# A linear-attention and mixture-of-experts kernel: logits for four blocks at once, routing in three parts, indirect transfers spread singly over the pairs, a PSUM bank of its own for each first-layer quarter

## The chip, the cores and the metric

The kernel runs on one core of a Trainium2 chip. The metric is the device time of one execution in microseconds (us). Three timed executions of the kernel before took 499.47, 500.51 and 506.63 us; the median is 500.51 us.

## The reference

Two stages follow each other. The first is causal linear attention with a decay per head, over 4 sequences of 768 tokens with 8 heads of 64. The second sends each of the 3072 tokens to the one of 8 experts with the highest logit, and weights what this expert gives by the softmax of that logit.

```
for b in range(nb):                       # blocks of 64 tokens
    intra = einsum('bhic,bhjc->bhij', qb, kb) * Dmask
    intra = einsum('bhij,bhjd->bhid', intra, vb)
    inter = einsum('bhid,bhde->bhie', qb * lam_pow, kv_state)
    out[:, :, sl] = intra + inter
    kv_state = lam_block * kv_state + einsum('bhsd,bhse->bhde', kb * rev_pow, vb)
logits = x @ w_gate + modality_bias[modality_id]
e_idx = argmax(logits, axis=1)
gate_w = softmax(logits)[arange(N), e_idx]
for e in range(E):                        # D = 512, F = 1024
    h = maximum(x[e_idx == e] @ w1[e], 0.0)
    out[e_idx == e] = gate_w[..., None] * (h @ w2[e])
```

With the inputs that are used, nearly all tokens go to two experts: 1319 to expert 3, 1494 to expert 6, 253 to expert 5 and 6 to expert 7.

## The kernel before

**Order.** The instructions of TensorE (PE), VectorE (DVE), ScalarE (ACT) and the queue engine SP stand in the order in which the program text issues them, and each engine executes its own in that order. GpSimd (POOL) has an order of its own that a list keeps (`pool(...)`). Indirect transfers are issued by POOL, one instruction per 128 rows.

**Attention.** The 24 blocks of 128 tokens go in 12 pairs, numbered m. For one pair PE computes `scores` (L245), the part from the running state (`from_state`, L284), the part from the values (`values`, L292), the update of the state (`products`, L257) and the logits (`gates`, L313). `gates` of one block issues 16 matmuls of 32 columns by 32 columns, each with a group of 32 tokens; a matmul on float32 shows as two records of the trace, so the two blocks of a pair show as x64.

**Routing.** The 24 blocks are routed in 4 parts of 6 blocks. For one part DVE transposes the logits (`lgt`, L326) and picks the expert (`choose`), PE counts ranks (`ranks`, L345 to L348), DVE works out slots (`slots_of`), and POOL scatters a record per token into a table `inv` in DRAM (`write_slots`, L375, one indirect transfer per block). After half of the tokens `count` (L383) and `early_list` fix two early tiles of 256 tokens; after all of them `late_list` fixes the rest.

**Experts.** A tile is 256 tokens of one expert. There are 2 early tiles, 2 thin tiles (64 and 32 tokens) and, with these inputs, 10 wide ones. For each tile SP fetches the tile's part of `inv` (`gidx`), POOL gathers the rows (`xg<-xs`, L551, 8 indirect transfers), DVE transposes them (`turn_rows`, L576), and ACT and DVE split rows and weights into a high and a low half (`split`, L524 and L525). `first_layer` has four quarters i of 24 matmuls (L588 to L590), each followed by a ReLU on ACT (`hh`, L606) and by the low half of its result on DVE (`hl`, L607). Two quarters share one PSUM tile `s` of two banks, of which there are two. `second` has 2 x 24 matmuls (L588 to L590, `o`), then ACT scales (`y`, L620) and POOL scatters the rows to the output (L621).

**The seam.** Behind the last pair the program issues `turn_rows` and `split_rows` of early tile 0, `choose` for the last part, the gathers of tile 1, the scatters, and then `first_layer` of tile 0. Its quarter 0 is followed by `rank_last`, which issues `ranks`, `slots_of`, the last scatters and `count`; quarters 1 to 3 stand behind them on PE. `keep_busy(18)` lets PE multiply zeros at the very start.

## Time and profile before

| | us |
|---|---|
| timed executions | 499.47, 500.51, 506.63 |
| profiled execution, device time | 502.24 |
| its span | 500.3 |
| PE busy | 404.7 (81%) |
| DVE busy | 265.1 (53%) |
| POOL busy | 218.3 (44%) |
| ACT busy | 204.7 (41%) |

The span is what the trace covers of the profiled execution; 1.94 us of its device time lie around it. Busy shares are means over stages that differ much. A matmul row of the timeline begins with its start; what stands in square brackets is the engine's idle time before it and what ended it, and "issue" is idle time for which the profile shows no wait.

### The profile page before, as it was taken

How to read it: one execution, taken by the hardware profiler on the slowest of the kernel's cores; microseconds unless marked ns; L12 is line 12 of the kernel's file. 1: busy time of each engine (PE TensorE's matmuls, PEld its weight loads, DVE VectorE, ACT ScalarE, POOL GpSimd, SP SyncE). 2: the span in 40 equal slices, each digit the busy share in tenths (PEclk: the TensorE clock that was granted, in tenths of full speed). 3: DMA queues.
4: the chain of work that ended last, by engine and by line, in shares of the span. 5: the costliest groups of instructions: out<-in, count | busy, mean ns of one | idle time of the engine just before them, and what ended most of it. 6: DMA issues, size and time to landing. Idle time of an engine off the chain costs nothing.

```text
span 500.3 us, 10978 instructions
## 1 busy us (share of the span) xinstructions
PE 404.7 (81%) x4118; PEld 353.8 (71%) x4118; DVE 265.1 (53%) x440; ACT 204.7 (41%) x385; POOL 218.3 (44%) x230
## 2 busy tenths in 40 slices
PE   8977887886518938958888889897979797989882
PEld 4867777775418838737777787787878787878871
DVE  4556667766134874206655545465656464747420
ACT  2744542661022512205444426354544444545320
POOL 1752555368725104561271808263635454450200
PEclk9998998996558969978999989899999999999998
DMA  7999992747100002940121856631111111010101
GB/s 262 400 411 409 412 412 89 256 96 246 37 8 2 22 22 36 284 153 10 12 63 19 262 154 202 182 82 42 33 53 23 63 20 67 17 63 3 43 3 38
DMA packets 39951, 62.67 MB, mean 125 GB/s; under 512 B 22730, under 2 KB 22732, under 8 KB 39888
## 3 DMA queue, kind: packets, MB, share of 16 engines
q1 hardware_dynamic: 29120, 42.83, 25.6%
q0 software_dynamic: 5936, 12.69, 7.9%
q10 hardware_dynamic: 4832, 6.36, 3.6%
q8 instruction: 34, 0.56, 0.5%
q14 instruction: 29, 0.24, 0.2%
HBM read 90.52 MB, written 13.67 MB: 208 GB/s over the span
## 4 chain that ended last, share of the span: by engine, by line
issue 39%; POOL 16%; DVE 4%; PE 4%; SPq 2%; DMA 2%; ACT 1%; another core or an unknown queue 1%; POOLq 1%; DVEq 0%; ACTq 0%
POOL xg L551 12%; POOL out_dram L621 4%; PE o L664 1%; SPq L536 1%; DVE w1l L525 1%; DMA xg<-xs,gidx 1%; PE s L588 1%; DMA gidx<-inv 1%; PE s L590 1%; PE s L589 1%; SPq L540 1%; POOLq L551 0%; DVE xt L576 0%; ACT w1h L524 0%
## 5 line engine op out<-in xcount | busy, mean ns | idle before, releaser
L551 POOL DMA_INDIRECT xg<-xs,gidx x80 | 99.1, 1239 | 118.7 <-DVE xt L576 90.0
L588 PE MATMUL s<-xh,w1h 128*128 128x256 f32 x384 | 115.8, 302 | 42.4 <-DVE hl L607 37.6
L589 PE MATMUL s<-xl,w1h 128*128 128x256 f32 x384 | 112.5, 293 | 2.0 <-issue 2.0
L588 PEld LDWEIGHTS s<-xh,w1h 128*128 128x128 f32 x384 | 77.3, 201 | 51.8 <-DVE hl L607 41.9
L590 PE MATMUL s<-xh,w1l 128*128 128x256 f32 x384 | 112.4, 293 | 0.5 <-issue 0.5
L525 DVE TENSOR_TENSOR w2l<-raw,w2h 128x1024 fp32r<-128x1024 f32 x48 | 58.8, 1225 | 38.4 <-ACT y L620 22.7
L590 PEld LDWEIGHTS s<-xh,w1l 128*128 128x128 f32 x384 | 77.5, 202 | 1.8 <-issue 1.8
L589 PEld LDWEIGHTS s<-xl,w1h 128*128 128x128 f32 x384 | 77.4, 201 | 1.9 <-issue 1.5
L606 ACT ACTIVATE hh<-s 128x512 fp32r<-128x512 f32 x48 | 28.7, 598 | 118.3 <-PE s L590 111.9
L607 DVE SCALAR_TENSOR_TENSOR hl<-s,hh 128x512 fp32r<-128x512 f32 x48 | 33.2, 691 | 80.4 <-ACT hh L606 76.2
L588 PE MATMUL o<-w2h,hh 128*128 128x512 f32 x192 | 75.0, 390 | 0.0
L590 PE MATMUL o<-w2h,hl 128*128 128x512 f32 x192 | 74.8, 390 | 0.0
L589 PE MATMUL o<-w2l,hh 128*128 128x512 f32 x192 | 74.7, 389 | 0.0
L525 DVE TENSOR_TENSOR w1l<-raw,w1h 128x1024 fp32r<-128x1024 f32 x48 | 57.0, 1247 | 2.8 <-issue 1.4
L524 ACT CAST w2h<-raw 128x1024 fp32r<-128x1024 f32 x48 | 49.8, 1037 | 0.0
L524 ACT CAST w1h<-raw 128x1024 fp32r<-128x1024 f32 x48 | 46.7, 1046 | 0.4 <-issue 0.4
L621 POOL DMA_INDIRECT out_dram<-y,idx x20 | 23.6, 1178 | 46.9 <-ACT y L620 42.0
L235 ACT ACTIVATE kd<-load,dk 128x64 f32<-128x64 f32 x160 | 39.6, 334 | 7.9 <-DVE state L274 3.8
L590 PEld LDWEIGHTS o<-w2h,hl 128*128 128x128 f32 x192 | 36.0, 188 | 7.7
L589 PEld LDWEIGHTS o<-w2l,hh 128*128 128x128 f32 x192 | 36.1, 188 | 7.1
L588 PEld LDWEIGHTS o<-w2h,hh 128*128 128x128 f32 x192 | 36.0, 188 | 7.0
L375 POOL DMA_INDIRECT inv<-pay,sloti x24 | 25.3, 1056 | 15.6 <-DVE sloti L368 9.2
(184 smaller groups left out, 467.0 us busy)
## 6 DMA issues: line engine op xcount, KB each, us to landing
raw<-in_w_dram SPq DMA_DIRECT2D x104, 512.0 KB
load<-in_qkv_dram SPq DMA_DIRECT2D x11, 2048.0 KB
xs<-xn ACTq DMA_DIRECT2D x24, 256.0 KB
both<-in_w_dram SPq DMA_DIRECT2D x8, 512.0 KB
load<-in_qkv_dram SPq DMA_DIRECT2D x4, 512.0 KB
xg<-xs,gidx POOLq DMA_INDIRECT x80
inv<-pad SPq DMA_DIRECT2D x2, 388.0 KB
gidx<-inv SPq DMA_DIRECT2D x40, 1.0 KB
```

Of the source, the lines that this page charges most:

```text
L235: nc.scalar.activation(out=kds[g][:, p, hl, :], in_=kn[:, p, hl, :], func=AF.Copy, scale=dk[:, hl, p, P - 1 : P])
L375: sc = nc.gpsimd.indirect_dma_start(out=inv, out_offset=bass.IndirectOffsetOnAxis(ap=at, axis=0), in_=pay[:, c, :], in_offset=None)
L524: nc.scalar.copy(out=hi, in_=src)
L525: nc.vector.tensor_tensor(out=lo, in0=src, in1=hi.bitcast(F32), op=ALU.subtract)
L536: nc.sync.dma_start(out=gidx[j * Q : (j + 1) * Q, :], in_=inv[bass.ds(vr, cols), 2 + j : 3 + j].rearrange("(t p) c -> p (t c)", p=Q))
L551: pool(nc.gpsimd.indirect_dma_start(out=to[:, t, :], out_offset=None, in_=xs[:rows, :], in_offset=bass.IndirectOffsetOnAxis(ap=gidx[:, t : ...
L588: nc.tensor.matmul(out, ah, bh, start=first, stop=False)
L589: nc.tensor.matmul(out, ah, bl, start=False, stop=False)
L590: nc.tensor.matmul(out, al, bh, start=False, stop=last)
L606: nc.scalar.activation(out=hh[a][:, b], in_=hp, func=AF.Relu)
L607: nc.vector.scalar_tensor_tensor(out=hl[a][:, b], in0=hp, scalar=0.0, in1=hh[a][:, b].bitcast(F32), op0=ALU.max, op1=ALU.subtract)
L621: sc = nc.gpsimd.indirect_dma_start(out=out, out_offset=bass.IndirectOffsetOnAxis(ap=idx[:, t, 0:1], axis=0), in_=y, in_offset=None, bound ...
```

## The change

1. **Banks.** In `first_layer` quarters 0 and 2 each take half of an `s` tile of their own, and quarters 1 and 3 go into the bank `kv` that the attention used for its state.
2. **Gates.** `gates` runs once per two pairs for four blocks, with 16 matmuls of 32 columns by 128 tokens.
3. **Routing.** 3 parts of 8 blocks instead of 4 of 6. DVE's routing work is recorded in a list (`put`) and issued at two places in a pair (`do`). The early tiles are fixed after 8 blocks; with these inputs they are one of expert 3 and one of expert 6, where both were of expert 3.
4. **Indirect transfers.** A table `aside` places the scatters and gathers singly or in twos behind parts of a pair.
5. **Seam.** `turn_rows` and `split_rows` of tile 0 move into the last pair. `rank_last` is spread over the first three quarters.
6. **Indices.** A tile's gather indices come from whole rows of `inv` of 32 bytes, two to a run, instead of single 4-byte words; DVE makes the indices from them by one exclusive or (`spread_idx`).
7. **Start.** `keep_busy(9)`, an early activation that loads ACT's table, the load of pair 1 in four transfers, and another order of the first pair. For the first block of a sequence POOL computes `kd` in one instruction instead of ACT in eight.
8. **Between the early tiles.** The four weight splits of tile 1 stand ahead of `late_list` (before, two stood ahead and two behind it); the index fetches and gathers that follow are reordered.

On PE, in the last stretch of pair m = 11 and the start of `first_layer` of tile 0, the rows of before are these (`x<-xt,wgq` are the gates, x15 means 15 equal rows, `s<-xh` opens the first quarter):

```order
L292 MATMUL o<-pt,load 64x128 x16
L313 MATMUL x<-xt,wgq 32x32 [waits Activation_49]
L313 MATMUL x<-xt,wgq 32x32 x15
L313 MATMUL x<-xt,wgq 32x32 [waits Activation_49]
L313 MATMUL x<-xt,wgq 32x32 x15
L588 MATMUL s<-xh_136,w1h 128x256 [waits Activation_49]
```

In the change an odd pair, here m = 5, ends like this, and an even pair has no gates (`kv<-load,kd` is the update of the state, `x<-ohsum,onesb` the count for the early tiles):

```order
L265 MATMUL kv<-load,kd 64x64 [waits Pool_49]
L265 MATMUL kv<-load,kd 64x64 x7
L265 MATMUL kv<-load,kd 64x64 [waits Activation_49] x8
L320 MATMUL x<-xt,wgq 32x128 [waits DVE_49]
L320 MATMUL x<-xt,wgq 32x128
L320 MATMUL x<-xt,wgq 32x128 [waits Activation_49] x2
L320 MATMUL x<-xt,wgq 32x128 x12
L402 LDWEIGHTS onesb
L402 MATMUL x<-ohsum,onesb 128x8 [waits DVE_49]
```

The 64 gate matmuls of two pairs have become 16 with four times the tokens.

On PE, in `first_layer` of a wide tile, these are the rows of before where quarter 1 begins and where quarter 3 begins, each with the last three rows of the quarter ahead (`s` is the shared PSUM tile):

```order
L588 MATMUL s<-xh_137,w1h 128x256
L589 MATMUL s<-xl_139,w1h 128x256
L590 MATMUL s<-xh_137,w1l 128x256
L588 MATMUL s<-xh_136,w1h 128x256 [waits DVE_49]
...
L588 MATMUL s<-xh_137,w1h 128x256
L589 MATMUL s<-xl_139,w1h 128x256
L590 MATMUL s<-xh_137,w1l 128x256
L588 MATMUL s<-xh_136,w1h 128x256 [waits DVE_49]
```

In the change the two places are these:

```order
L622 MATMUL s<-xh_143,w1h 128x256
L623 MATMUL s<-xl_145,w1h 128x256
L624 MATMUL s<-xh_143,w1l 128x256
L622 MATMUL kv<-xh_142,w1h 128x256 [waits PE_49,Activation_49]
L623 MATMUL kv<-xl_144,w1h 128x256
...
L622 MATMUL s<-xh_143,w1h 128x256
L623 MATMUL s<-xl_145,w1h 128x256
L624 MATMUL s<-xh_143,w1l 128x256
L622 MATMUL kv<-xh_142,w1h 128x256 [waits DVE_49]
```

Quarter 1 no longer waits for DVE; quarter 3 does, and what it waits for there is quarter 1's `hl`, since both use `kv`.

On POOL, from pair m = 9 to behind the attention, before (`qd` and `faded` are work of the attention, `xg<-xs` gathers, `inv<-pay` scatters):

```order
L551 DMA xg<-xs,gidxA_143 128x128 x2
L265 TENSOR_TENSOR faded<-state_126,pq 128x256
L226 TENSOR_TENSOR qd<-load,pq 128x512 x2
L551 DMA xg<-xs,gidxA_143 128x128 x6
L375 DMA inv<-pay,sloti 24832x8 x3
L551 DMA xg<-xs,gidxA_145 128x128 x8
L375 DMA inv<-pay,sloti 24832x8 x9
```

and in the change, from pair m = 9 on:

```order
L585 DMA xg<-xs,gidx_1296 128x128 x2
L273 TENSOR_TENSOR faded<-state_131,pq 128x256
L585 DMA xg<-xs,gidx_1296 128x128
L273 TENSOR_TENSOR faded<-state_132,pq 128x256
L230 TENSOR_TENSOR qd<-load,pq 128x512
L585 DMA xg<-xs,gidx_1296 128x128
L230 TENSOR_TENSOR qd<-load,pq 128x512
L585 DMA xg<-xs,gidx_1296 128x128 x2
L394 DMA inv<-pay,sloti 24832x8 x4
L585 DMA xg<-xs,gidx_1637 128x128 x8
L394 DMA inv<-pay,sloti 24832x8 x12
```

All gathers of tile 0 now stand ahead of the last pair; behind them 4 scatters, the 8 gathers of tile 1 and 12 scatters still follow each other without other work between.

The core of the diff:

```diff
-SOON = B - 2
+RN = 3
+RC = B * NC // RN
-        def gates(g):
-            xt = xts.pop(g)
+        def gates(grp):
+            four = range(4 * grp, 4 * (grp + 1))
             for p in range(NP):
-                for t in range(4):
-                    nc.tensor.matmul(lps[b % 2][t * Q : (t + 1) * Q, c, :], wgq[:, g % HB, p, :], xt[:, p, t * Q : (t + 1) * Q],
+                for t, g in enumerate(four):
+                    nc.tensor.matmul(lps[t * Q : (t + 1) * Q, grp % 2, :], wgq[:, g % HB, p, :], xts[g][:, p, :],
                                      start=(p == 0), stop=(p == NP - 1), tile_position=(0, t * Q))
...
+        def spare():
+            return ps.tile([P, HB, NP, D], F32, name="kv", bufs=1).rearrange("p c a d -> p (c a d)")
         def first_layer(between=lambda i: None):
             for i in range(4):
                 a, b = divmod(i, 2)
-                if b == 0:
-                    hp2 = ps.tile([P, 2, 2, TT], F32, name="s", bufs=2)
-                hp = hp2[:, b]
+                hp = spare() if b else ps.tile([P, 2, NP, P], F32, name="s", bufs=2)[:, 0].rearrange("p a t -> p (a t)")
+                hp = hp.rearrange("p (a t) -> p a t", a=2)
...
-        few = {4: 2, 5: 4, 7: 2, 8: 4, 11: 3}
-        keep_busy(18)
+        aside = {5: (0, 0, 2), 6: (1, 1, 1), 7: (1, 1, 1), 8: (0, 0, 1), 9: (1, 2, 1), 10: (1, 1, 1)}
+        keep_busy(9)
...
+            elif m == pairs - 1:
+                write_slots(RC // 2)
+                split(raw1[:, 2], w1h[:, 2], w1l[:, 2])
+                turn_rows()
+                split_rows()
+            do(3)
...
-            for g in (a, b):
-                gates(g)
+            if m % 2:
+                gates(m // 2)
...
         store(B * NC - 1)
-        turn_rows()
-        split_rows()
-        routed = B - 1, *choose(B - 1)
+        routed = RN - 1, *choose(RN - 1)
         fetch_w1(*fetch_regs(1))
         fetch_rows(1)
-        write_slots(3)
+        write_slots(RC)
...
         def rank_last(i):
             if i == 0:
+                do()
+            elif i == 1:
                 ranks(routed[-1])
                 slots.extend(slots_of(*routed))
-                write_slots(NC)
+                do()
+                write_slots(RC)
+            elif i == 2:
                 count()
...
         first_layer(rank_last)
         fetch_w2(*fetch_regs(1))
         turn_rows()
         split_rows()
-        split_w1(range(2))
+        split_w1()
         late_list(exA, nA)
-        split_w1(range(2, 4))
+        do()
         fetch_w1(*fetch_regs(thins))
+        for t in range(2):
+            second(0, t)
         for n in range(thins, wides + 1):
             fetch_idx(n)
-        for t in range(2):
-            second(0, t)
```

## Rows read from the trace of the kernel before

**Rows 1.** Stretches: start:end, length, busy us (records) PE, PEld, DVE, ACT, POOL, clock, DMA.

```profile
0.00:119.20 119.20, 99.15 (x2156) 84.93 (x2160) 77.82 (x164) 57.87 (x191) 61.69 (x98) 0.95 0.83 306
119.20:161.90 42.70, 22.03 (x171) 19.29 (x170) 13.34 (x29) 7.40 (x11) 24.64 (x23) 0.63 0.12 35
161.90:227.00 65.10, 51.08 (x360) 40.55 (x358) 29.72 (x92) 18.97 (x27) 24.45 (x24) 0.87 0.33 101
227.00:490.80 263.80, 232.46 (x1443) 208.97 (x1440) 144.21 (x157) 119.78 (x156) 106.51 (x84) 0.98 0.24 68
490.80:500.30 9.50, 0.00 (x0) 0.00 (x0) 0.00 (x0) 0.69 (x1) 0.98 (x1) 0.74 0.07 23
```

**Rows 2.** PE's waits in the wide tiles, 227 to 491: us, times, longest.

```profile
PE s L588 <- DVE hl L607: 27.2, 18, 2.2
```

**Rows 3.** PE's timeline in one wide tile: start, duration, operation, idle before.

```profile
255.06 0.28 PE L588 MATMUL s<-xh,w1h 128*128 128x256 f32 x1
...
259.52 0.39 PE L588 MATMUL s<-xh,w1h 128*128 128x256 f32 x1 [1.47 <-DVE hl L607]
...
266.92 0.38 PE L588 MATMUL s<-xh,w1h 128*128 128x256 f32 x1 [1.47 <-DVE hl L607]
...
269.85 0.40 PE L588 MATMUL o<-w2h,hh 128*128 128x512 f32 x1
...
280.76 0.28 PE L588 MATMUL s<-xh,w1h 128*128 128x256 f32 x1
```

**Rows 4.** DVE's timeline in the same tile, quarter 0's `hl`.

```profile
258.78 0.69 DVE L607 SCALAR_TENSOR_TENSOR hl<-s,hh 128x512 fp32r<-128x512 f32 x1 [0.64 <-issue]
```

**Rows 5.** Groups by line in the wide tiles, POOL's gathers: busy, mean ns, idle.

```profile
L551 POOL DMA_INDIRECT xg<-xs,gidx x64 | 82.7, 1292 | 107.1 <-DVE xt L576 90.0 <-issue 17.1
```

**Rows 6.** Attention, 26 to 76: the columns of rows 1.

```profile
26.00:76.00 50.00, 40.59 (x1039) 36.61 (x1036) 31.62 (x65) 25.55 (x90) 24.27 (x32) 0.97 1.03 410
```

**Rows 7.** DMA queues there: packets, MB, share of 16 engines; instruction fetches.

```profile
q8 instruction: 9, 0.15, 1.2%
```

**Rows 8.** PE's waits in the attention, 8 to 119, the largest.

```profile
PE x L313 <- issue: 4.7, 7, 1.9
```

**Rows 9.** PE's timeline, the first pair's work.

```profile
18.21 1.09 PE L284 MATMUL o<-qd,state 64*64 64x128 f32 x16
...
22.06 0.76 PE L313 MATMUL x<-xt,wgq 128*32 128x32 f32 x64
```

**Rows 10.** PE's timeline behind the last pair.

```profile
119.15 0.66 PE L313 MATMUL x<-xt,wgq 128*32 128x32 f32 x32
...
129.72 0.58 PE L588 MATMUL s<-xh,w1h 128*128 128x256 f32 x1
...
139.60 0.43 PE L590 MATMUL s<-xh,w1l 128*128 128x256 f32 x1
145.62 0.20 PE L345 MATMUL x<-oh,lowb 128*128 128x48 bf16 x1 [5.59 <-DVE oh L339]
...
149.65 0.56 PE L588 MATMUL s<-xh,w1h 128*128 128x256 f32 x1
```

**Rows 11.** POOL's timeline there, the first and the last of 22 indirect transfers.

```profile
113.74 1.84 POOL L551 DMA_INDIRECT xg<-xs,gidxA  x1 [0.16 <-issue]
...
140.53 0.96 POOL L375 DMA_INDIRECT inv<-pay,sloti  x1 [0.31 <-issue]
```

**Rows 12.** DVE's timeline there, in `late_list` and behind it.

```profile
143.74 0.38 DVE L326 STREAM_TRANSPOSE lgt<-x 128x192 f32<-128x192 f32 x1 [16.19 <-remote]
...
169.09 0.15 DVE L388 COPY cntB<-x 1x8 f32<-1x8 f32 x1
...
179.07 0.14 DVE L521 CAST nums<-many 1x1 int32<-1x1 f32 x1
179.15 2.36 DVE L525 TENSOR_TENSOR w1l<-raw,w1h 128x1024 fp32r<-128x1024 f32 x2
```

**Rows 13.** POOL's timeline, the first gather of tile 4.

```profile
195.80 1.00 POOL L551 DMA_INDIRECT xg<-xs,gidx  x1 [3.38 <-DMA gidx<-inv]
```

More of the change, by code (lines that the diff above doesn't have):

```diff
@@ L321, in t2, with put, do @@
         def t2(nm, dt=F32):
-            return work.tile([P, NC], dt, name=nm, bufs=1)
+            return work.tile([P, RC], dt, name=nm, bufs=1)
+        todo = []
+        def put(what, *args, **kw):
+            todo.append((what, args, kw))
+        def do(n=None):
+            for what, args, kw in todo[:n]:
+                what(*args, **kw)
+            del todo[:n]
         def choose(b):
-            lgt = work.tile([P, NC, WG], F32, name="lgt", bufs=1)
-            nc.vector.transpose(out=lgt, in_=lps[b % 2])
@@ L364, in slots_of @@
             sm = t2("sm")
[L365 to L369 removed]
+            put(nc.vector.tensor_reduce, out=sm, in_=l, axis=AX, op=ALU.add)
@@ L371, in linear_attention_moe @@
+            put(nc.vector.tensor_scalar, out=sm, in0=sm, scalar1=1e-9, scalar2=None, op0=ALU.add)
+            put(nc.vector.reciprocal, out=pay[:, cs, 1].bitcast(F32), in_=sm)
+            put(nc.vector.tensor_tensor, out=sloti, in0=slot, in1=m8s, op=ALU.add)
+            return [(b * RC + c, sloti[:, c : c + 1]) for c in range(RC)]
         slots = []
```

368 lines of the change are left out of this document (205 added, 163 removed).

## The prediction

> **What bounds the kernel now.** I read the stretches first, to see which engine fills which part of the span, then PE's waits in the longest stretch, then timelines where PE stands still. The stretches [rows 1] divide the span at 119.2 us (end of the attention's values), 161.9 (first `second` of early tile 0), 227.0 (first wide tile) and 490.8 (last matmul). PE is busy for 99.15 of 119.20 us, then for only 22.03 of 42.70 at a granted clock of 0.63, then 51.08 of 65.10, then 232.46 of 263.80 at 0.98. So four questions: why PE idles 20 us in the attention, what the 42.7 us at the seam are, what follows from the middle, and what the wide tiles lose.
>
> In the wide tiles one wait stands out: 18 times, 27.2 us together, PE's first matmul of a quarter waits for DVE's `hl` [rows 2]. In one tile it is seen twice [rows 3]: quarter 0 begins at 255.06, quarter 1 at 259.52, quarter 3 at 266.92, `second` at 269.85, the next tile at 280.76. That is 25.70 us. Quarter 1 begins just behind the `hl` of quarter 0, which runs from 258.78 for 0.69 [rows 4]: the two quarters share a tile of PSUM, so the later one waits for the reader of the earlier one. POOL is no bound there: 64 gathers took 82.7 us of the stretch, 1.29 us each [rows 5]; eight, and two scatters of like length, with gaps of 0.3 (as in rows 11, below), are 16 us of a tile.
>
> In the attention PE has work for 40.59 of 50 us [rows 6] while the DMA engines are full (410 GB/s). In that time the busier of the instruction queues, which I take for PE's, had 9 fetches [rows 7], one in 5.6 us. The largest idle time of PE there is put down to "issue", 4.7 us ahead of gates [rows 8], so to no wait that the profile shows. From the gates of the first pair, 22.06 [rows 9], to those of the last, 119.15 [rows 10], eleven pairs take 97.1 us, 8.83 each; by the 81% of rows 6 that is 7.17 of work and 1.66 of idle.
>
> At the seam the last pair's gates begin at 119.15, and quarter 0 of tile 0, which stands right behind them, at 129.72; 64 records that took 0.76 us in the first pair [rows 9] take 10 us, and the 24 matmuls of quarter 0 another 9.9 (to 139.60) [rows 10]. Meanwhile POOL runs 22 indirect transfers without a break, 113.74 to 141.5 [rows 11], 1.26 us each. DVE's `lgt` then starts at 143.74, after 16.19 us of idle [rows 12], though the gates it reads were done by 130. `ranks` waits for it (145.62), and quarter 1 behind `ranks` starts at 149.65 [rows 10]. So this run delays PE twice: in what it issues and in what it reports.
>
> **The change part by part.**
>
> *Banks (wide tiles).* Quarters of 24 matmuls at the spacing inside one take 24 x 0.1177 = 2.83 us (the second half of the tile: 269.85 - 266.92 = 2.93 with the slow first one). Quarter 0 to quarter 1 took 4.46, so a wait costs 1.64, two a tile 3.27 [rows 3]. In the change quarter 1 waits for nothing on DVE. Quarter 3 waits for `hl` of quarter 1: `hl` of quarter 0 ends at 259.47, 4.41 after the tile's start [rows 4]; one quarter later is 7.24, and quarter 3 would start at 3 x 2.83 = 8.49, so 1.25 us are to spare. A tile becomes 4 x 2.83 + 10.91 = 22.2, with a little for boundaries 22.3; ten are 223 against 263.8. Three of the ten tiles of before were longer than 25.7 (the mean is 26.38), with the clock down; if that excess stays, and only 3.27 a tile goes, it is 231. I take 224, since the clock dips follow the waits: **-40** (-33 to -41.5).
>
> *Gates.* 64 matmuls per two pairs become 16. By rows 6 a pair of 8.83 us has 2075 x 8.83/50 = 366 records on PE, loads and matmuls; of the 64 for gates' matmuls 48 go, and as many loads: 270 are left in the mean. The gates' own time is 0.76 a pair; the nearest row for the new form, 16 records of 64x128 in 1.09 [rows 9], doubled for two pairs' 32 records, bounds it at 1.09 a pair, and 32 records at the old gates' pace are 0.19 a pair. So the work of a pair is 6.6 to 7.5; nearer to the lower end since the moving width, not the contraction, is what changed: 6.8. If the idle 1.66 stays too, a pair is 8.45 and the eleven win 4.2. If idle goes with the number of instructions, 8.83 x 270/366 = 6.5 is under the work, so the work bounds: 6.8, 22 won. Loads don't forbid it: at rows 6 a pair's 2 MB come each 6.1 us or faster. I take 7.5 a pair, nearer to the lower end because the idle is "issue" and no engine's: -14.6. The start (half the warm-up, ACT's table loaded earlier, finer first loads) is bounded by 3; its loads arrive no sooner, so I count -0.5. Together **-15** (-3 to -23).
>
> On the instructions the Trainium skill speaks against this. Runtime: NRT & Kernel Launch, section Instruction fetch mechanics, says that an engine's instructions come in blocks of 256 and that crossing a block is "mostly hidden"; by it, fewer instructions win only their own time. That would be -4 here, a rival below. The trace's nine fetches in 50 us [rows 7] do not decide it.
>
> *Seam.* Behind the change `turn_rows` and `split_rows` lie in the last pair, the gates are 16 matmuls, and `ranks` stands behind quarter 1. POOL still has 16 transfers in a row (4, 8, 4) from the last pair on, 16 x 1.26 = 20 us, and 8 more behind the ranks. Lower end: no stall, four quarters of 2.83, gates, 2 us for the rows: 14. Upper end: the run holds PE as before. It starts some 7.5 us ahead of the pair's end, so 13 us are left; at 9.9 us a quarter PE does 1.3 quarters in them; `lgt` follows 2.2 us behind the run (143.74 - 141.5), the choice and ranks 1.9 (145.62 - 143.74); then 2.7 quarters at 2.83 or, at half the clock, at 5.65: 25 to 32. I take 24, nearer to the upper end, since a long run without a break is what rows 10 and 11 show. 42.7 - 24 = **-19** (-10 to -28.5).
>
> *Routing parts, spread transfers, POOL's keys, `spread_idx`.* The same 24 scatters and 8 gathers a tile; more of the gathers lie in the pairs, beside PE's work. Of these runs the cost in the attention is inside its idle. Routing in three parts removes a third of small DVE and PE work at 0.14 to 0.38 us an instruction [rows 12], off the path except at the seam, where it is counted. DVE gets one exclusive or per tile, of the order of 0.2 us, in a tile of which it works 14.4 (144.21 for ten [rows 1]), so 8 of 22.3 stay idle; if that cover were gone, 2 us in all.
>
> *Between the early tiles.* The two splits that stood behind `late_list` (the list 169.09 to 179.07, the splits 2.36 us [rows 12]) now stand ahead of it, so the list is ready 2.4 us later, and with it the index fetches and the first gather of tile 4 (195.80 [rows 13]). `spread_idx` and DVE's place behind other work add a microsecond; tile 1 is of another expert now, so 4 MB of weights, and as many for a thin tile, come again, 20 us at 410 GB/s, in a stretch whose DMA share is 0.33 [rows 1]. What it wins (quarter 1 of tile 1 no longer waits for `hl`) ends in the same wait for rows. **+3** (0 to +8).
>
> *Tail.* 9.50 us as before [rows 1].
>
> Sum: -40 - 15 - 19 + 3 = -71. The span of 500.3 becomes 429.3; the profiled execution's device time was 502.24, 1.94 more, so 431.2. It lay 1.7 over the median of the runs (500.51), so the median should be **430**. The forecast's own range is 416 to 443: the attention alone at its bad end is +12, the seam alone +9, both near their good ends together -14.
>
> **Rivals.**
>
> *Fewer instructions win only their own time.* The attention wins 4 instead of 15: 441. For it: the idle could be the scatters beside small matmuls, as at the seam, and there are no fewer of them. Against it: idle falls on all three kinds of matmul, also where POOL scatters nothing. 0.2.
>
> *The seam only moves.* POOL's run, now begun earlier, slows the last pair too, and the last eight scatters run beside the quarters, so that the seam and last pair give back 12: 442. For it: the gates of the last pair show this slowing [rows 10]. Against: matmuls of the wide tiles run beside gathers at full pace. 0.12.
>
> *The tile waits elsewhere.* If `hl` of quarter 1 comes over 1.25 us later than worked out, because ACT or DVE hold other work (`y`, the next rows, `w2l`), quarter 3 waits again; with half of the win lost, -24 in place of -40: 446. Against: DVE's work per quarter, a split of 1.18 [rows 12] and an `hl` of 0.69, fits in 2.83, and ACT has less in the stretch (119.78 against 144.21 us [rows 1]). 0.09.
>
> *Slower.* PE slowed by indirect transfers in every wide tile: at the seam 24 matmuls took 9.9 us beside POOL's run, 3.5 times their time. Now PE's waits leave gaps in a tile; without them POOL's 13 us of transfers would lie beside matmuls alone. At that pace 13 us do 3.7 us of work, a tile becomes 22.3 + 9.3 = 31.6, ten are 316, +52 in place of -40: 522. It decides from a tile of 30.5 us on: ten are then 305, 41 more than before, against 31 won in front. Against it: in the tile shown PE kept 0.118 a matmul beside the gathers [rows 3, 5]. 0.04.
>
> **How the numbers follow.** Forecast 0.55, rivals 0.2, 0.12, 0.09 and 0.04. About 2% is what a measurement of this kernel can tell from no change. Only the last is not faster by over 2%, and with it a mishap of the seam together with the tile might come within 2%: faster 0.95, same 0.01, slower 0.04. The range holds the forecast's own from 414 and the three mild rivals up to 450; below and above I leave 0.15.
>
> **What would show it.** PE's waits for `hl` gone from the wide tiles, starts of tiles 22.3 apart: the banks. Gates of odd pairs x32 in about 0.8 us, pairs 7.5 apart: the gates; at 8.4 the first rival. `second` of tile 0 near 128 and `lgt` just behind POOL's sixteen: the seam. Starts of the first wide tile 68 behind `second` of tile 0: the middle. Wrong is the forecast if tiles stand over 24 apart, or if the first `second` comes after 140.

## The result, and the profile after

The changed kernel took 446.0, 440.96, 447.0 and 447.27 us, a median of 446.5 us, beside 500.12 us for the kernel before in the same runs: a ratio of 0.888 (95% interval 0.878 to 0.898). The forecast was 430 in a range of 414 to 450. The profiled execution has a span of 444.2 us, 56.1 less than before; the sum had said 71 less.

The stretches of the changed kernel, cut at the same places of the program as [rows 1] (end of the attention's values, first `second` of tile 0, first wide tile, last matmul); the columns are those of [rows 1]:

```profile
0.00:105.60 105.60, 93.53 (x1597) 80.41 (x1597) 74.43 (x147) 48.72 (x157) 64.07 (x97) 0.94 0.92 346
105.60:135.14 29.54, 19.98 (x139) 17.93 (x139) 15.86 (x32) 8.96 (x13) 19.49 (x19) 0.77 0.55 170
135.14:206.24 71.10, 52.92 (x361) 40.88 (x359) 29.92 (x96) 18.90 (x27) 32.79 (x30) 0.90 0.47 161
206.24:434.60 228.36, 226.10 (x1443) 205.23 (x1440) 143.30 (x164) 119.00 (x156) 105.12 (x84) 1.00 0.26 79
434.60:444.20 9.60, 0.12 (x1) 0.00 (x0) 0.00 (x0) 0.69 (x1) 0.98 (x1) 0.68 0.08 27
```

| stretch | before | after | difference | forecast |
|---|---|---|---|---|
| attention | 119.2 | 105.6 | -13.6 | -15 |
| seam | 42.7 | 29.5 | -13.2 | -19 |
| middle | 65.1 | 71.1 | +6.0 | +3 |
| ten wide tiles | 263.8 | 228.4 | -35.4 | -40 |
| tail | 9.5 | 9.6 | +0.1 | 0 |

All four terms have the forecast's sign, and each falls short of it by 1.4 to 5.8 us; together that is the 15 us between 429.3 and 444.2. How far one pair of traces can be trusted shows in a second pair, taken later and on one chip, `b_same` and `a_same2` (told below): there the four differences are -10.7, -9.3, +1.6 and -33.2 us. The signs hold; the sizes move by up to 4.4 us. PE is busy for 226.1 of 228.4 us in the wide tiles now. The five largest waits of PE (line, what is waited for, us in total, times, longest):

```profile
PE o L623 <- DVE w2l L544: 7.6, 1, 7.6
PE kv L622 <- DVE hl L644: 5.8, 9, 3.5
PE x L364 <- DVE m L340: 4.0, 1, 4.0
PE x L320 <- ACT xt L303: 3.8, 1, 3.8
PE o L292 <- DVE state L280: 2.9, 1, 2.9
```

In the wide tiles the 27.2 us of [rows 2] have become 2.3, in eight of the ten; the other 3.5 of these 5.8 us fall on tile 1:

```profile
PE kv L622 <- DVE hl L644: 2.3, 8, 0.3
```

The waits of 7.6, 4.0 and 3.8 us are new: the first in the middle, the other two at the seam. One wide tile of the changed kernel, the first matmul of each quarter, of `second` and of the next tile, beside [rows 3]:

```profile
251.58 0.28 PE L622 MATMUL s<-xh,w1h 128*128 128x256 f32 x1
...
254.46 0.28 PE L622 MATMUL kv<-xh,w1h 128*128 128x256 f32 x1
...
257.34 0.28 PE L622 MATMUL s<-xh,w1h 128*128 128x256 f32 x1
...
260.64 0.39 PE L622 MATMUL kv<-xh,w1h 128*128 128x256 f32 x1 [0.26 <-DVE hl L644]
...
263.59 0.40 PE L622 MATMUL o<-w2h,hh 128*128 128x512 f32 x1
...
274.51 0.28 PE L622 MATMUL s<-xh,w1h 128*128 128x256 f32 x1
```

A tile is 22.93 us, down from 25.70. Quarter 1 no longer waits; quarter 3, which should have had 1.25 us to spare, waits 0.26. With that wait, it is 3.30 us from the start of quarter 2 to the start of quarter 3, where the other quarters take 2.88.

### The profile page after: what moved, and what is told of

It reads as the page before. It is cut to its first block, busy times and chain, and to the rows that moved or that the text cites. A ratio compares the mean times of both kernels' runs of the same rounds, so it can differ in the third digit from the quotient of the medians.

```text
span 444.2 us, 9748 instructions
## 1 busy us (share of the span) xinstructions
PE 392.7 (88%) x3532; PEld 344.5 (78%) x3532; DVE 263.5 (59%) x437; ACT 196.3 (44%) x353; POOL 222.5 (50%) x229
## 4 chain that ended last, share of the span: by engine, by line
issue 39%; POOL 17%; DVE 5%; DMA 5%; another core or an unknown queue 3%; SPq 2%; ACT 1%; POOLq 0%; DVEq 0%; ACTq 0%
POOL xg L585 13%; POOL out_dram L658 4%; DMA both<-in_w_dram 2%; DMA raw<-in_w_dram 2%; DVE w2l L544 1%; DVE w1l L544 1%; DVE hl L644 1%; SPq L600 0%; ACT w1h L543 0%; DMA found<-inv 0%; SPq L567 0%; ACT xh L543 0%; SPq L605 0%; DVE xt L610 0%
## 5 line engine op out<-in xcount | busy, mean ns | idle before, releaser
L585 POOL DMA_INDIRECT xg<-xs,gidx x96 | 115.2, 1200 | 95.0 <-DVE xt L610 66.3
L544 DVE TENSOR_TENSOR w2l<-raw,w2h 128x1024 fp32r<-128x1024 f32 x48 | 58.7, 1223 | 35.8 <-ACT w2h L543 24.5
L622 PE MATMUL kv<-xh,w1h 128*128 128x256 f32 x192 | 56.6, 295 | 5.8 <-DVE hl L644 5.8
L623 PE MATMUL s<-xl,w1h 128*128 128x256 f32 x192 | 55.6, 289 | 1.1 <-issue 1.1
L624 PE MATMUL s<-xh,w1l 128*128 128x256 f32 x192 | 55.8, 291 | 0.3 <-issue 0.3
L623 PE MATMUL kv<-xl,w1h 128*128 128x256 f32 x192 | 55.7, 290 | 0.0
L624 PE MATMUL kv<-xh,w1l 128*128 128x256 f32 x192 | 55.5, 289 | 0.0
L622 PE MATMUL s<-xh,w1h 128*128 128x256 f32 x192 | 55.4, 288 | 0.0
L622 PEld LDWEIGHTS kv<-xh,w1h 128*128 128x128 f32 x192 | 37.8, 197 | 8.0 <-DVE hl L644 7.7
L643 ACT ACTIVATE hh<-kv 128x512 fp32r<-128x512 f32 x24 | 14.4, 598 | 57.0 <-PE kv L624 29.2
L624 PEld LDWEIGHTS s<-xh,w1l 128*128 128x128 f32 x192 | 37.3, 194 | 1.8 <-issue 1.8
```

Source lines behind the costliest of these rows:

```text
L544: nc.vector.tensor_tensor(out=lo, in0=src, in1=hi.bitcast(F32), op=ALU.subtract)
L585: pool(nc.gpsimd.indirect_dma_start(out=to[:, t, :], out_offset=None, in_=xs[:rows, :], in_offset=bass.IndirectOffsetOnAxis(ap=gidx[:, t : ...
L622: nc.tensor.matmul(out, ah, bh, start=first, stop=False)
L623: nc.tensor.matmul(out, ah, bl, start=False, stop=False)
L624: nc.tensor.matmul(out, al, bh, start=False, stop=last)
L643: nc.scalar.activation(out=hh[a][:, b], in_=hp, func=AF.Relu)
```

## The experiments

Three questions were open: whether each large part carries its stretch by itself, what holds up the seam and the middle, and why a wide tile is 22.9 and not 22.3. The runs fall into three groups. Those of one group ran on one chip, beside the kernel before: `b_banks`, `a_gates32`, `a_thinlate` and `a_same`, where the kernel before took 496.21 us; `a_dummy`, `a_early`, `a_norun` and `a_mid`, where it took 479.00; `b_same`, `a_same2`, `a_lump` and `a_best`, where it took 497.49. Runs of different groups are compared stretch by stretch in their traces, or by their ratio to the kernel before of their own group. That the chips differ turned out to matter, and is told where it does.

**The banks alone.** The kernel before, with this edit (and the lines that define `spare` and give the thin tiles the same shape of `s`):

```diff
-                if b == 0:
-                    hp2 = ps.tile([P, 2, 2, TT], F32, name="s", bufs=2)
-                hp = hp2[:, b]
+                hp = spare() if b else ps.tile([P, 2, NP, P], F32, name="s", bufs=2)[:, 0].rearrange("p a t -> p (a t)")
+                hp = hp.rearrange("p (a t) -> p a t", a=2)
```

> The kernel before with the banks of the change alone: quarters 0 and 2 in a tile s each, quarters 1 and 3 in kv. Theory (the banks carry the wide tiles' gain by themselves): the ten wide tiles take 228 to 232 us as in the changed kernel (228.4) instead of 263.8, tile starts 22.9 apart; tiles 0 and 1 win 2 to 4 us more, so about 462 to 466 us. Rival (the gain in the wide tiles needs the other parts too, for instance the index fetches in one piece): tiles stay over 24 us apart, 475 us or more. Both: the attention and the seam stay as in the kernel before, 119 and 43 us.

Measured: 459.78 us, the kernel before 496.21 (ratio 0.927, 0.922 to 0.932). The ten wide tiles, with the columns of [rows 1]:

```profile
220.40:447.90 227.50, 224.47 (x1444) 203.61 (x1440) 141.84 (x156) 117.99 (x155) 107.29 (x84) 1.00 0.27 79
```

227.5 us, as in the changed kernel (228.4). So the banks make the wide tiles' gain by themselves: 36.3 us against the first trace of the kernel before, 34.1 against its second (261.6, in `b_same`). The first wide tile also starts earlier, at 220.4 us (227.0 and 222.9 in those two).

**The gates back to many small matmuls.** The changed kernel, each gate matmul of 128 columns cut into four of 32, at the same place:

```diff
-            for p in range(NP):
-                for t, g in enumerate(four):
+            for u in range(4):
+                us = slice(u * Q, (u + 1) * Q)
+                for p in range(NP):
+                    for t, g in enumerate(four):
-                    nc.tensor.matmul(lps[t * Q : (t + 1) * Q, grp % 2, :], wgq[:, g % HB, p, :], xts[g][:, p, :],
+                        nc.tensor.matmul(lps[t * Q : (t + 1) * Q, grp % 2, us], wgq[:, g % HB, p, :], xts[g][:, p, us],
```

> The changed kernel with 64 gate matmuls of 32 by 32 columns per two pairs instead of 16 of 32 by 128: the instruction count of the kernel before, at the places of the change. Theory (the attention's idle on PE went with the number of instructions): a pair in the middle of the attention goes from 6.9 back to 8 to 8.8 us, the attention ends 10 to 15 us later, 456 to 461 us. Rival 1 (only the gates' own time counts, 0.76 a pair against 0.53): the attention ends 2 to 4 us later, 449 us. Rival 2 (the idle went because of the order of DVE's and POOL's work): no change within 2 us.

Measured: 465.56 us against 446.61 for the unchanged one in the same group. The attention's values end at 125.1 instead of 104.9 us, 20 later, more than the theory's 10 to 15. Its stretch from 26 to 76 us, the same stretch as [rows 6]:

```profile
26.00:76.00 50.00, 40.83 (x1052) 37.26 (x1051) 32.42 (x61) 21.20 (x73) 23.80 (x24) 0.93 1.03 411
```

and that of the changed kernel:

```profile
26.00:76.00 50.00, 47.92 (x990) 43.22 (x992) 40.79 (x87) 25.27 (x84) 30.17 (x31) 1.00 1.03 411
```

With the small gates PE is busy for 40.83 of 50 us, as in the kernel before (40.59); without them 47.92. The number of records that PE gets through is about the same in all three (2075, 2103, 1982), and the DMA engines are as full. PE's waits with the small gates, from 8 to 125 us:

```profile
PE x L322 <- issue: 6.6, 9, 2.6
PE o L292 <- issue: 5.9, 5, 2.7
PE kv L265 <- issue: 2.3, 4, 1.1
```

The idle that no wait explains is back, and it also stands ahead of other work than the gates (`o`, `kv`), as here:

```profile
38.55 1.13 PE L292 MATMUL o<-qd,state 64*64 64x128 f32 x16 [2.69 <-issue]
```

POOL's first indirect transfer in this run begins at 67.36 us; by then the `scores` of pair 6 (59.99 us, 52.78 in `a_same`) are already 7.2 us later than there. So transfers beside small matmuls, which the prediction's first rival named, do not make this part of the loss. The gates' own time differs by about 0.2 us a pair. So without the wide gates nothing of the attention's gain is left (125.1 us, 119.2 before). Whether they would bring it into the kernel before by themselves was not run, and this edit changes the number of matmuls and their width together.

**More matmuls that feed nothing.** To tell the number of instructions from the form of the gates, and a full DMA from a quiet one:

```diff
+            if m in (3, 8):
+                for i in range(192):
+                    nc.tensor.matmul(small_ps[: Q, 400:408], nought[:, :Q], nought[:, :8], start=True, stop=True)
```

> The changed kernel with 192 more matmuls of zeros (float32, 32 weights columns, 8 moving columns, into unused columns of PSUM) at the end of pair 3 and again of pair 8; they feed nothing. Pair 3 ends while the DMA engines are full with loads (near 38 to 45 us), pair 8 in the first quiet stretch of the DMA engines (near 80 us). Their own time, by 64 gate matmul records in 0.76 us, is about 4.6 us for 384 records. Theory (with the DMA engines full, PE gets no more than the 42 records of matmuls and loads in a us that the kernels with many small gates showed, 2075 and 2103 in 50 us): the first set and the pair behind it show idle times of 1.4 to 2.7 us put down to issue, together some 10 us more than the second set, which runs at its own pace. Rival (idle belongs to the gates themselves, to their groups of 32 columns and their reader on DVE): both sets run at their own pace, with no issue idle around them.

Measured, on PE's timeline:

```profile
45.59 5.29 PE L840 MATMUL x<-nought 128*32 128x8 f32 x123
51.94 13.88 PE L840 MATMUL x<-nought 128*32 128x8 f32 x258 [1.06 <-issue]
...
103.19 18.95 PE L840 MATMUL x<-nought 128*32 128x8 f32 x384
```

A miss for both theories: a record took 0.043 and 0.054 us in the first set and 0.049 in the second, four times what a gate record takes [rows 9], so the sets took 20.1 and 19.0 us, with 1.06 us of idle in the first and none in the second (465.89 us for the whole, in one execution). Part of the factor four is the clock. A stretch at the start of each set and a later one, with the columns of [rows 1]:

```profile
45.60:47.00 1.40, 1.40 (x50) 1.40 (x48) 0.10 (x1) 0.51 (x3) 1.22 (x2) 1.00 1.04 423
54.00:58.00 4.00, 4.00 (x79) 4.00 (x78) 0.00 (x0) 0.00 (x0) 0.00 (x0) 0.50 1.03 410
103.20:105.00 1.80, 1.80 (x60) 1.80 (x58) 0.00 (x0) 1.01 (x3) 0.00 (x0) 1.00 0.18 16
107.00:110.00 3.00, 3.00 (x60) 3.00 (x60) 0.59 (x2) 0.86 (x4) 2.64 (x4) 0.50 0.26 49
```

At a granted clock of 1.00 (2.4 GHz) a record takes 0.028 and 0.030 us, at 0.50 (1.2 GHz) 0.051 and 0.050; the gates of [rows 9] ran at 1.00. The clock fell in both sets although PE never stood still in the second. The DMA engines make no difference: their share is 1.04 and 0.18 in the first pair of figures, 1.03 and 0.26 in the other. What is left, 2.4 times a gate record at the same clock, may be PE's pace for a long row of small matmuls, or that of writing the same few columns again and again, where the gates go round four groups of columns; the run doesn't tell which. So that gates cut small cost the time is shown by the run before; why is open.

**The transfers in a row.**

```diff
-        aside = {5: (0, 0, 2), 6: (1, 1, 1), 7: (1, 1, 1), 8: (0, 0, 1), 9: (1, 2, 1), 10: (1, 1, 1)}
+        aside = {5: (0, 0, 2), 6: (0, 0, 3), 7: (0, 0, 3), 8: (0, 0, 1), 9: (0, 0, 4), 10: (0, 0, 3)}
```

> The changed kernel with the indirect transfers of pairs 6, 7, 9 and 10 together at the end of the pair (3, 3, 4 and 3 in a row) instead of singly or in twos behind its parts. Theory (the spreading matters: a run of transfers in a row holds up PE or POOL's own work that the next pair waits for): the attention's values end 3 to 8 us later than in the unchanged one, with new waits of PE for qd or faded of POOL, or issue idle, in pairs 6 to 10. Rival (the gain of the attention is that of the gates alone): the values end within 1.5 us of the unchanged one.

Measured: 453.14 us against 447.75 for the unchanged one in the same group. The values end at 107.2 instead of 104.8, between the two expectations; the larger part comes behind them, where PE's gates wait for ACT as the rows of tile 0 come later:

```profile
116.98 2.40 PE L320 MATMUL x<-xt,wgq 128*32 128x128 f32 x28 [9.48 <-ACT xt L303]
```

The same row waits 5.51 in the unchanged kernel of that group. The seam is 36.6 us long instead of 30.4: 4.0 us of that are this wait, and `hh` of quarter 0 is later too (8.6 us behind its quarter instead of 6.2). So the spreading is worth about 5 us by the medians, and most of it by the earlier rows of tile 0, which neither theory had named.

**The order at the seam.** `turn_rows` and `split_rows` of tile 0 behind the last copies of `xt`, and the choice ahead of the first quarter:

```diff
                 split(raw1[:, 2], w1h[:, 2], w1l[:, 2])
-                turn_rows()
-                split_rows()
...
             else:
                 turn(b)
+            if m == pairs - 1:
+                turn_rows()
+                split_rows()
...
         routed = RN - 1, *choose(RN - 1)
+        do()
```

> The changed kernel with two moves at the seam: turn_rows and split_rows of tile 0 stand behind the last pair's copies of xt instead of ahead of them, and the choice of the last part's experts stands ahead of the first quarter instead of behind it. In the changed kernel the last gates waited 3.8 us for ACT's copy of xt, which stood behind the split of the gathered rows, and the ranks waited 4.0 us for the choice. Theory 1 (the order on ACT and DVE made both waits): gates at 107, quarter 0 at 110 or 111, lgt behind them near 112, ranks without a wait, first second product at 127 to 130 instead of 135 to 137, time 439 to 442 us. Theory 2 (PE's report of finished work is held while POOL issues its run of indirect transfers, so the choice can't start earlier wherever it stands): lgt not before 119, the ranks still wait, the second product at 133 to 135, time 444 to 446 us.

The rows at stake, in the changed kernel on ACT:

```profile
108.18 0.62 ACT L543 CAST xh<-xt 128x512 fp32r<-128x512 f32 x1 [3.39 <-DVE xt L610]
...
109.22 1.06 ACT L303 COPY xt<-o 128x512 f32<-128x512 f32 x2
...
119.59 0.60 ACT L643 ACTIVATE hh<-s 128x512 fp32r<-128x512 f32 x1 [4.36 <-PE kv L624]
```

The last copies of `xt` stand on ACT behind the split of the gathered rows, so PE's gates wait 3.8 us for them; that wait the change itself made. And `hh` of quarter 0 starts at 119.59, though that quarter's last matmul ended at 116.0.

Measured: 429.89 us, with 479.00 for the kernel before in that group (ratio 0.894, 0.886 to 0.902), no different from the changed kernel's ratios in the other groups (0.888, 0.901, 0.904). On this chip the seam of `a_mid`, whose seam is that of the changed kernel, is 24.5 us, and here it is

```profile
103.90:126.00 22.10, 16.65 (x141) 15.46 (x140) 16.71 (x34) 8.79 (x13) 17.53 (x16) 0.85 0.71 232
```

that is 2.4 us less, with `lgt` at 112.24 and the ranks without a wait, as theory 1 had it. Less was to be won here than theory 1 thought: in `a_mid` the ranks waited 0.46 us only, and in place of the gates (7.3 us in `a_mid`) quarter 0 now waits, 5.1 us for ACT's `xh`. In `a_best`, below, the same two moves on another chip gave 29.7 instead of 30.4 us. There too `lgt` came at 112.16 and the ranks had no wait, so what theory 2 expected of `lgt` failed on both chips; but `hh` of quarters 0 and 1 started 2.3 and 6.7 us behind their quarters, so the lateness that theory 2 spoke of is there, at another place than it looked.

**POOL's run taken away.**

```diff
-        fetch_rows(1)
-        write_slots(RC)
...
                 do()
-                write_slots(RC)
+                write_slots(2 * RC)
+                fetch_rows(1)
```

> The changed kernel with POOL's run at the seam taken away: behind the four scatters of the last pair come no transfers until the last ranks are known; then 12 scatters and the 8 gathers of tile 1. Theory 2 (POOL's run holds PE at the seam): hh of quarter 0 within 0.5 us of the quarter's end, ranks without a wait, quarter 2 in 2.9 us instead of 7.0, the first second product at 125 to 128 instead of 135. The rows of tile 1 come some 12 us later than in the changed kernel, so the first quarter of tile 1 starts near 157 instead of 147 and the whole is 5 to 10 us slower. Rival (the seam is bound by DVE's and ACT's order): the first second product stays at 133 or later.

Measured on the same chip as the one above: the seam is 23.7 us, with the run 24.5; the rows of tile 1 come later and the whole is 452 us in one execution. On a chip that shows no late `hh`, then, taking POOL's run away wins less than 1 us, and what theory 2 expected of `hh` and the ranks holds there with the run as well (`hh` 0.03 us behind quarter 0, the ranks waiting 0.46 us in `a_mid`). On the other chips the edit wasn't tried. One run shows something near it: in `a_gates32` the last gates took so long that quarter 0 ended at 148.6 us, behind POOL's run (which ended at 141.9), and `hh` followed 0.04 us later; in `a_same` on the same chip, with the run beside quarter 0, it followed 6.4 us later. That speaks for the run as the cause, though the gates differ between the two as well.

**The middle.** First the three `spread_idx` behind quarter 3 of tile 1:

```diff
         def find_thin(i):
-            if i == 2:
+            if i == 3:
```

> The changed kernel with the three spread_idx of the thin tiles and tile 4 behind quarter 3 of tile 1 instead of behind quarter 2. In the changed kernel the second product of tile 1 waits 7.6 us for the last w2l, which stands on DVE behind these three, and they wait for index fetches that land at 166 to 173. Theory (that wait is on the path): the wait is gone, the second product of tile 1 ends near 174 instead of 183.5, the fetch of the next w2 starts some 9 us earlier too, and the first wide tile starts 5 to 8 us earlier: 439 to 441 us. Rival (the gathered rows of the thin tiles and the weights set the start of the wide tiles anyway): PE waits later instead, ahead of the thin tiles, and the time stays within 2 us of the changed kernel.

Measured: 443.94, 445.15, 452.33 and 453.55 us, the unchanged one in the same group 446.02, 446.16, 447.05 and 450.81; the traced executions are those of 445.15 and 447.05. The 7.6 us wait is gone and the first thin tile starts at 173.2 instead of 185.1, but the first wide tile at 205.0 instead of 206.9; PE waits at another place:

```profile
PE s L674 <- DMA both<-in_w_dram: 8.1, 4, 6.7
```

From the first `second` of tile 0 on the middle is 70.6 us long, 70.2 in the unchanged one. So the rival was right: the wait of 7.6 us was real and cost nothing. Then, with it, the fetch that this wait names moved forward, and `turn_rows` ahead of the next `spread_idx`:

```diff
         fetch_w1(*fetch_regs(thins))
+        both1 = w1_part("both1", F32)
+        fetch_w1(*fetch_regs(thins + 1, True), to=both1)
         for t in range(2):
             second(0, t)
...
-        spread_idx(wides + 1)
         turn_rows()
+        spread_idx(wides + 1)
```

> The changed kernel with three moves between the early tiles: the spread_idx of the thin tiles behind quarter 3 of tile 1, the w1 of the second thin tile fetched right behind that of the first, ahead of the index fetches and in the time in which the DMA engines are quiet, and turn_rows of tile 4 ahead of the spread_idx of tile 5. The first move alone brought PE's second product 10 us forward and the first wide tile only 1 or 2 us, since PE then waited 8.1 us for that w1. Theory (the middle is bound by the weights that come again for the thin tiles and by the order of their fetches): that wait goes, the first wide tile starts at 197 to 200 instead of 206, time 438 to 441 us. Rival (the transposed rows and the small products of the thin tiles are a chain of their own): the first wide tile starts at 203 to 206.

Measured: 435.82 us with 479.00 for the kernel before (ratio 0.905, 0.897 to 0.913). The middle is 71.3 us long, in `a_early` of the same group, where it is that of the changed kernel, 67.7: worse by 3.6. The issue of that fetch waited until 157.7 us for a buffer that tile 1 still used, and the index fetches behind it on SP came later; PE's largest waits are then

```profile
PE x L685 <- ACT hn L678: 9.0, 1, 9.0
PE s L674 <- DVE xf L610: 5.0, 1, 5.0
```

The first wide tile starts at 200.3, next to the theory's number, but only because the seam is shorter on this chip; by its own length the middle is on the far side of the rival. The third try, with the seam's two moves and `spread_idx` of the thin tiles behind quarter 3 as above:

```diff
+        do()
...
-        spread_idx(wides + 1)
-        turn_rows()
         for t in range(2):
             second(1, t)
-        fetch_rows(wides + 1)
...
-        split_rows()
...
         hnt = thin_turn(hns[0])
+        turn_rows()
+        spread_idx(wides + 1)
+        fetch_rows(wides + 1)
+        split_rows()
         thin_second(thins, hnt, raw2)
```

> The changed kernel with the two moves of the seam (turn_rows and split_rows of tile 0 behind the last copies of xt, the choice ahead of the first quarter) and with the middle reordered: the spread_idx of the thin tiles behind quarter 3 of tile 1, and the transposes, the split and the next gathers of tile 4 behind the first thin tile's transposes. Theory (the middle is bound by ACT's and DVE's order: the thin tile's activation stood on ACT behind the split of tile 4's rows, 9.0 us in one trace): against the unchanged kernel in the same call the seam is 2 to 6 us shorter, the middle 3 to 6 us, together 6 to 11 us. Rival (the gathered rows of tile 4 set the start of the wide tiles whatever stands in front): the middle stays within 1.5 us and the whole wins 2 to 5 us.

Measured: 445.06 us against 447.75 in the same group, ratios to the kernel before 0.896 (0.887 to 0.906) and 0.904 (0.896 to 0.911): no difference that can be told. The middle is 71.2 us (69.3 in the unchanged one). None of the three orders has a shorter middle than the unchanged one beside it (70.6 and 70.2, 71.3 and 67.7, 71.2 and 69.3), and each has another wait on PE, 7 to 9 us long. What they share is the chain from `late_list` over three sets of index fetches on SP, the gathers, and the weights that come again for tile 1 and the thin tile; I take that chain for the bound, but none of the runs removed it. No version was found that beats the changed kernel measurably.

**The two kernels again.** The changed kernel was run again twice, and the kernel before once with its trace.

> The changed kernel again, beside the others on the same chip: both theories expect 441 to 447 us, with the attention's values done near 105.6 us, the first second product near 135 and the first wide tile near 206.

> The changed kernel again, on the same chip as the two that follow. If the kernel before is near 498 here: 446 us, first second product near 135 to 137, wide tiles 22.9 apart. If it is near 479: 432 to 436 us, with the first second product near 129, wide tiles 22.4 apart, and hh of the second quarter within 0.5 us of the quarter's end in every wide tile, where the first trace of the changed kernel showed 1.7 us. Rival: the wide tiles wait at quarter 3 on either chip.

> The kernel before again, with its trace, on the chip of this call. In one earlier call the kernel before took 496 us (median of 7), in another 479. Theory (chips differ in how far POOL's runs of indirect transfers hold PE up, and in little else): if this call's median for the kernel before is near 479, the stretch from the attention's values to the first second product is 25 to 33 us instead of 42.7, the gates of the last pair take under 3 us instead of 10, and the wide tiles stay at 25.7 us or a little less; if it is near 498, the stretch and the gates repeat the trace of before within 3 us. Rival: a chip that is faster is faster everywhere by the same few per cent.

Measured: 446.61 and 447.75 us for the changed kernel with 496.21 and 497.49 for the one before, so the ratio repeats (0.901 and 0.904). In the group of `a_early`, `a_mid`, `a_norun` and `a_dummy` the kernel before took 479.00 (477.72 to 483.08 in seven executions). `b_same` fell on a chip near 497.5 and repeats the trace of before within 4 us a stretch (attention, seam, middle, wide tiles):

```profile
0.00:115.50 115.50, 96.52 (x2152) 81.99 (x2152) 76.07 (x163) 57.75 (x191) 60.19 (x98) 0.99 0.83 308
115.50:155.20 39.70, 19.94 (x170) 17.90 (x170) 14.66 (x31) 7.62 (x12) 25.45 (x24) 0.70 0.19 63
155.20:222.90 67.70, 51.63 (x361) 41.12 (x359) 30.85 (x92) 20.03 (x28) 24.21 (x24) 0.85 0.32 97
222.90:484.50 261.60, 230.86 (x1444) 207.38 (x1440) 143.27 (x156) 118.70 (x155) 106.67 (x84) 0.99 0.24 68
```

In `a_same2` the four are 104.8, 30.4, 69.3 and 228.4 us. So what the faster chip does to the kernel before was not seen in a trace. It is not faster everywhere by the same share, which the rival had: the changed attention's values end at 103.9 to 105.1 us there in `a_early`, `a_mid` and `a_norun`, at 104.8 to 105.6 in the three traces of the changed kernel on the other chips. What it does to the wide tiles of the changed kernel is seen in `a_mid`:

```profile
200.30:424.70 224.40, 224.40 (x1444) 205.05 (x1440) 144.68 (x164) 119.75 (x156) 105.20 (x85) 1.00 0.26 81
```

PE is busy for all of 224.4 us and waits for nothing. In that run `hh` of quarter 1 starts when the quarter ends (the tile began at 245.11, and quarter 1 ended at 251.02); POOL's scatter is shown with it:

```profile
250.72 1.22 POOL L658 DMA_INDIRECT out_dram<-y,idx  x1 [0.31 <-issue]
251.12 0.60 ACT L643 ACTIVATE hh<-kv 128x512 fp32r<-128x512 f32 x1 [1.35 <-PE kv L624]
```

while in the first trace of the changed kernel eight of ten tiles look like this one, which began at 251.58 and whose quarter 1 ended near 257.5:

```profile
257.19 1.26 POOL L658 DMA_INDIRECT out_dram<-y,idx  x1 [0.31 <-issue]
259.26 0.60 ACT L643 ACTIVATE hh<-kv 128x512 fp32r<-128x512 f32 x1 [2.98 <-remote]
```

In these eight tiles `hh` starts 1.76 to 1.83 us behind the end of the quarter's last matmul, which the profile models, and 0.10 us or less behind it in the other two. So it is in eight of ten tiles of each run of the two groups with the longer times (1.69 to 2.04 us over `b_banks`, `a_gates32`, `a_thinlate`, `a_same`, `a_same2`, `a_lump` and `a_best`), and in no tile of the four runs of the third (0.10 us at most). In the program `hh` waits for PE's last matmul, and in the prompt tiles the profile names it; in the late ones it says "remote". So I take it that PE's report comes late. When it does, a transfer of POOL stands across the end of the quarter, 5.9 us into the tile: in the first trace the scatter runs from 5.6 to 6.9 us in the eight late tiles, from 4.3 to 5.5 in the first tile, and in the last tile none runs then. On the third chip the scatter stands at the same place (5.6 to 6.8) and `hh` is prompt. So both are needed, the transfer and the chip; what in the chip it is, no run shows. The late `hh` makes a late `hl`, and with 1.25 us to spare quarter 3 then waits. A tile is 22.93 us with it and 22.44 without (`a_mid`), which is nearly all of the 4.4 us by which the wide tiles missed the forecast's 224.

## Why the prediction was right, and where it was short

*Banks: right, in mechanism and within 4.4 us.* The forecast was 224 us; the trace shows 228.4, the banks alone 227.5, and one chip 224.4. That the clock dips would go with the waits came true: the ten tiles ran at a granted clock of 1.00, where the three long ones of before had 0.94. The step that was off is quarter 3's wait on `hl` of quarter 1: the 1.25 us of slack was worked out right, but the work assumed that PE's end is known to ACT at once, and `hh` started 1.8 us later. The trace of before had shown such a delay at the seam, and a small one in two of its three long tiles, 0.7 us at quarter 0, with a gather of POOL across the quarter's end (near 283.76 here):

```profile
283.43 1.34 POOL L551 DMA_INDIRECT xg<-xs,gidx  x1 [0.30 <-issue]
284.42 0.60 ACT L606 ACTIVATE hh<-s 128x512 fp32r<-128x512 f32 x1 [1.79 <-PE s L590]
```

The prediction put these tiles down to the clock. The rival of the tile that waits elsewhere named the place, quarter 3, but for another reason (other work on ACT or DVE), and had 1.6 us a tile where 0.5 were lost.

*Gates and attention: right, -13.6 for -15.* In the stretch 26 to 76 PE is busy for 95.8% of the time, and between 19.4 and 81.3 us nine pairs take 6.9 us each; the work of a pair had been put at 6.8 and the pace at 7.5. The last pairs gave some of it back: the tenth waits 2.9 us for DVE's `state`, and the last two take 12 us each. Even so the attention takes 16.3 us less from the values of pair 1 to its end, more than the 14.6 forecast. The term that was mis-sized is the start: it was put at -0.5 and cost 2.7 us, as these values begin later (before, then after):

```profile
25.77 1.53 PE L292 MATMUL o<-pt,load 128*64 128x128 f32 x24
28.51 1.97 PE L300 MATMUL o<-pt,load 128*64 128x128 f32 x32
```

Two sizes on the way were off without harm: the wide gates take 1.36 us for two pairs, where the sign to look for was about 0.8, and 2 MB at 410 GB/s are 5.1 us, not 6.1. The rival that fewer instructions win only their own time is refuted by the small gates, which lost 20 us for some 0.2 us a pair of own time. The prediction weighed a sentence of the Trainium skill (Runtime: NRT & Kernel Launch, Instruction fetch mechanics: crossing a block of 256 instructions is "mostly hidden") against it. By it the loss of the small gates would be, as an estimate, their 0.2 us a pair, some 2 us in all; the runs here show 20. Whether fetching is what costs them, no run here shows.

*Seam: sign right, short by 5.8.* 29.5 us, near the upper end of the forecast's 14 to 32 where 24 was taken. Two things were in it. `hh` of the first quarter 3.6 us late, and quarter 2 taking 7.2 us at a granted clock of 0.56, are the upper end's mechanism:

```profile
123.10:130.30 7.20, 5.70 (x31) 4.87 (x27) 2.61 (x7) 2.61 (x4) 2.73 (x3) 0.56 0.26 75
```

POOL's transfers stood beside only the first half of that quarter (the last of them ended at 126.4); the half clock, by which the prediction had a quarter at 5.65 instead of 2.83, is the larger part of what it took over. The 3.8 us ahead of the gates are not: moving `split_rows` into the last pair put it ahead of ACT's copies of `xt`, and the prediction, which counted what the moved work no longer delays, did not ask what stands behind it on ACT. On the chip with prompt reports the seam is 24.5 us (`a_mid`), the forecast's 24; that is luck, since 7.3 us of it are this wait of the gates. Of the rival by which the seam only moves, 12 us given back, the seam shows about half.

*Middle: sign right, short by 3.* It took 71.1 us where 68.1 was forecast. The wait of 7.6 us behind `spread_idx` on DVE was not named, but the run without it shows that its removal does not shorten the middle (70.6 us against 70.2). The weights that come again were put aside as lying in a quiet stretch; with the first wait gone PE stood still for just those (8.1 us), so that step was too easy.

*Slower-side rival: refuted.* Matmuls of the wide tiles keep 0.12 us each beside ten gathers and scatters a tile.

The measured 446.5 us lies nearer to the mild rivals' 441, 442 and 446 than to the 430 of the forecast, and in its range only by 3.5 us. No rival is what happened as a whole: all four terms came out a little worse than taken, and the range had room for that.

## What to carry to other kernels

When two parts of a pipeline share a buffer of several PSUM banks, give each its own bank: here the gain could be read from the wait times the number of times it recurs, with the clock dips that go with it, and came in by itself to 10 to 15% (36.3 and 34.1 us for 40). Many small matmuls can cost far more than their busy time (20 us here for some 0.2 us a pair), and the mark of it was idle put down to issue that stands ahead of whatever comes next. When work is moved to an earlier place, look at what it now stands in front of on each in-order engine, and how long it waits there for its own input.

## What was not expected of the hardware

Chips of the same kind gave the same kernel 479.0 us (seven executions, 477.7 to 483.1) and 496.2 to 500.1 us in other groups. The traces of the changed kernel show one thing that differs: on the chips of the longer times ACT's `hh` starts 1.8 us behind a finished quarter of PE in eight of ten wide tiles, and up to 9.4 us behind it at the seam, where POOL runs an indirect transfer as the quarter ends; on the other chip it is prompt in every wide tile with the same transfer at the same place. Whether that makes up all of the 18 us was not measured.

A row of matmuls with 8 moving columns, all into the same columns of PSUM, took 0.030 us a record at a granted clock of 1.00 and 0.050 at 0.50, where the gates with 32 columns into different ones took 0.012 at 1.00 (0.76 us for 64). Full DMA engines made it no slower, and the clock fell to 0.50 under it while PE had no idle.
